# Idle transposes ahead of an attention kernel, replaced by full-float products in six tile forms

## The chip, the cores and the metric

The kernel runs on one core of one Trainium2 chip. The time is device microseconds of one execution. A core has TensorE (PE, the matrix array, with weight loads PEld), VectorE (DVE), ScalarE (ACT), GpSimd (POOL) and SyncE (SP, which issues DMAs here); each has its own queue of instructions.

## The reference

A pre-layernorm block on x of 2048 rows by 512: attention with 32 heads of 16, one key and one value head for all of them, and then a gated FFN of width 1792.

```
x  = A_x
q  = (LN(x) @ wq) in 32 heads of 16;  k = LN(x) @ wk;  v = LN(x) @ wv      # one k, one v
p  = softmax(q k^T / 4);  o = p v;   h  = x + concat(o) @ wo
h2 = h + (gelu(LN(h) @ w_gate) * (LN(h) @ w_up)) @ w_down
```

All inputs and the output are float32.

## The kernel before, in words

Rows are handled as 16 tiles of 128 (index t) and as 4 blocks of 512 (index b). The program has two parts.

The **prologue** (function `prologue`) makes keys, values and the first queries. For each tile t it goes round several engines:

- `stats(t)`: mean and variance on VectorE, the factor and shift from them by three small operations on GpSimd;
- `normalize(t)`: ScalarE writes xn, the normalised tile;
- `turn(t)`: TensorE transposes xn in four pieces of 128x128 into a PSUM tile `pt`; ScalarE copies it to `xT_hi` in a rounded float type (float32r), VectorE writes the rest of the rounding to `xT_lo`;
- `project_k` and `project_q` (through the generators `q_first` and `q_rest`): products of xT with the weights, in three terms (hi hi, lo hi, hi lo), into `pk` and `pq`.

`stats` runs three tiles ahead of `turn` and `normalize` two. Instructions of TensorE, GpSimd, ScalarE and, in the prologue, VectorE are queued in the order in which the code is written, so a place in the code is a place on the engine's queue. The list `IDLE` says how many *idle transposes* stand ahead of the turns of tiles 0 to 6: `turn(t)` first issues `IDLE[t]` transposes of the identity matrix into the same `pt`, whose result the real transposes then overwrite. After the sixteen turns come the last k projections, bounds for the softmax (`norm_k`, `max_k`), and the remaining q projections. Queries go through a DRAM array `q_d` to `qg_first`.

The **main part** scores 2048 keys against 512 queries of four heads at a time: `scores` makes s from kaug and qg (50 rows; the two matmuls of a step sit in rows 0 and 64 of the array), ScalarE takes the exponential p, and `weigh` adds p times v into `acc`, four heads on four column tiles of 32. p and v are plain float32 there; most other products have float32r operands. Later projections and the FFN are woven in between, as products on the two row halves of the array.

PSUM has eight banks of 512 floats; in the prologue `psum1` deals them out in turn (`width = 8`). `ident` is the 128x128 identity in float32, made on GpSimd; `v_sb` is a float32 array of 128x512 which VectorE fills with ones at the start and into which `leave_v` later writes v.

Of the kernel before, what the change touches and what calls it, by code (L numbers as in the profile page):

```python
# [19 lines left out]
P = 128  # L20
# [12 lines left out]
AHEAD_W = 2  # L33

LAST_Q = 258

LAG = 6

# [24 lines left out]
def kernel(  # L63
# [12 lines left out]
    nc = tc.nc  # L76
# [30 lines left out]
    ident = const.tile([P, P], F32, name="ident")  # L107
# [6 lines left out]
    v_sb = const.tile([P, KC, 2 * DH], F32, name="v_sb")  # L114
# [53 lines left out]
    def run(outer, first):  # L168
# [226 lines left out]
        if first:  # L395
            set_banks("ps_pro")
            width = 8
            order = tc.manual_schedule(engines={mybir.EngineType.DVE})
            with order:
                qg_first = prologue(  # L400
                    psum1, xT, wq_hi, wq_lo, sel, k2m, q_first, q_rest, advance,
                    first_q, first_bound, fill_first, eb
                )
# [670 lines left out]
        with tc.manual_schedule(engines={mybir.EngineType.SP, mybir.EngineType.DVE}):  # L1074
# [6 lines left out]
            while n < lead:  # L1081
# [6 lines left out]
                elif r < 30:  # L1088
                    kinds, runs = MIXED[r % 10]
                    if kinds == "ss" and 10 * left > 13 * (LAST_Q - n):  # L1090
                        kinds = "sm"
                    elif kinds == "mm" and 10 * left < 11 * (LAST_Q - n):
                        kinds = "sm"
                else:
                    kinds, runs = ("mm" if 10 * left > 13 * (LAST_Q - n) else "sm"), 1
                rest, held = token == REST, False
# [151 lines left out]
    def prologue(psum1, xT, wq_hi, wq_lo, sel, k2m, q_first, q_rest, advance, first_q, first_bound, fill_first, eb):  # L1248
        with ExitStack() as pro:
# [61 lines left out]
            nc.vector.memset(zero.bitcast(F32), 0.0)  # L1311
            nc.sync.dma_start(q_d[:, 3 * DH + 1, :].bitcast(F32), zero.bitcast(F32))

            def stats(t):
                st = sb.tile([P, 6], F32, tag="st", bufs=4, name=f"st_1_{t}")
                mv = sb.tile([P, 2], F32, tag="mv", bufs=4, name=f"mv_1_{t}")
                nc.vector.bn_stats(st, xs[t])
                nc.vector.bn_aggr(mv, st)
                rstd = sb.tile([P, 1], F32, tag="rstd", bufs=4, name=f"rstd_1_{t}")
                nc.gpsimd.tensor_scalar(rstd, mv[:, 1:2], EPS, None, op0=ALU.add)  # L1320
                nc.gpsimd.tensor_tensor(rstd, rstd, power[:, 0:1], op=ALU.pow)
                sh = sb.tile([P, 1], F32, tag="shift", bufs=4, name=f"shift_1_{t}")
                nc.gpsimd.tensor_scalar(
                    sh, mv[:, 0:1], rstd, -1.0, op0=ALU.mult, op1=ALU.mult
                )
                return sh, rstd
# [6 lines left out]
            def turn(t, xn):  # L1333
                pt = psum1(f"pt_{t}").rearrange("p (c q) -> p c q", c=DC)

                for k in range(IDLE[t] if t < len(IDLE) else 0):
                    nc.tensor.transpose(pt[:, k % DC, :], ident, ident)
# [59 lines left out]


            AHEAD, FIRST_FROM = 2, 6
            IDLE = (28, 3, 8, 9, 8, 12, 14)  # L1400
            sums, xns, pks, kss, vTs, pns, pvs = {}, {}, {}, {}, {}, {}, {}
            for t in range(AHEAD + 1):
                sums[t] = stats(t)
            for t in range(AHEAD):
                xns[t] = normalize(t, *sums.pop(t))
            for t in range(NT):
                if t + AHEAD + 1 < NT:
                    sums[t + AHEAD + 1] = stats(t + AHEAD + 1)
# [158 lines left out]
```

## Time and profile before

| | |
|---|---|
| timed runs | 1410.52 and 1411.73 us, median 1411.12 |
| profiled execution: span from first to last instruction | 1408.1 us (the page gives no time of its own around it) |
| mean granted TensorE clock | 0.996 |
| instructions | 25648 |
| TensorE busy | 1391.7 us, 99% |
| ScalarE busy | 1041.2 us, 74% |
| VectorE busy | 552.7 us, 39% |
| GpSimd busy | 189.4 us, 13% |

How the views read: a timeline row gives start, length, engine, line, operation, what it writes and from what, its shape and how many are merged (x28), and in brackets the engine's idle time just before it and what ended that. A chain row gives start, length and what the chain went through. A row of groups ends in busy time and mean nanoseconds of one. A row of windows gives a stretch, its length, and busy time of each engine with a count, then the granted clock (1.00 is full), the DMA engines' share and GB/s. A matmul on part of the array reads "50*128" for rows by columns.

### The profile page before, as it was taken

What the parts mean: (1) busy time and instruction counts of PE and PEld (TensorE: products, weight loads), DVE (VectorE), ACT (ScalarE), POOL (GpSimd) and SP (SyncE); (2) the same over time, 40 slices, a digit from 0 to 9 for tenths busy, and PEclk for the clock granted to TensorE, in tenths of its full rate; (3) what the DMA queues carried; (4) which work ended last, traced back from release to release, by engine and by line L of the source; (5) the groups of instructions that cost most, each with busy time, mean ns of one, the idle gap of its engine ahead of it and who ended that gap; (6) DMA issues with size and microseconds to landing.
All of it is one profiled execution on the core that took longest, in us unless ns stands there. A gap on an engine that the chain in (4) does not pass through costs nothing.

```text
span 1408.1 us, 25648 instructions
## 1 busy us (share of the span) xinstructions
PE 1391.7 (99%) x10646; PEld 782.7 (56%) x10646; DVE 552.7 (39%) x982; ACT 1041.2 (74%) x1149; POOL 189.4 (13%) x288
## 2 busy tenths in 40 slices
PE   8999999999999999999999999999999999999998
PEld 7433333335555555555555655555555555557886
DVE  7322323333342434333252433424352342427665
ACT  7699999996777787777787777777787777772000
POOL 6655565501000000000000000001000000002000
PEclk9999999999999999999999999999999999999999
DMA  4578777842341322233252332223242241335551
GB/s 160 162 238 273 236 243 243 298 134 91 126 150 53 124 106 102 73 112 122 84 169 72 117 118 87 87 100 111 99 151 97 88 147 56 134 124 198 181 199 59
DMA packets 85041, 194.52 MB, mean 138 GB/s; under 512 B 9904, under 2 KB 24240, under 8 KB 84884
## 3 DMA queue, kind: packets, MB, share of 16 engines
q1 hardware_dynamic: 77484, 167.39, 35.3%
q0 software_dynamic: 7264, 25.30, 5.0%
q8 instruction: 86, 1.41, 0.4%
q14 instruction: 39, 0.32, 0.1%
q10 hardware_dynamic: 168, 0.10, 0.0%
HBM read 142.93 MB, written 49.55 MB: 137 GB/s over the span
## 4 chain that ended last, share of the span: by engine, by line
PE 93%; ACT 3%; DMA 1%; issue 1%; DVE 1%; POOL 0%; SPq 0%; ACTq 0%; DVEq 0%; POOLq 0%
PE acc L439 33%; PE s L431 19%; PE pu L949 9%; PE pg L949 8%; PE pd L949 4%; PE pq L429 4%; PE pd L626 3%; ACT p L435 3%; PE pd L648 3%; PE pg L648 3%; PE pu L648 3%; PE pp L626 2%; PE pp L757 1%; DMA x<-in_A_x_dram 1%; PE pxt L693 1%
## 5 line engine op out<-in xcount | busy, mean ns | idle before, releaser
L435 ACT ACTIVATE p<-s 128x1024 f32<-128x1024 f32 x1024 | 969.7, 1030 | 224.6 <-PE s L431 220.1
L439 PE MATMUL acc<-p,v_sb 128*32 128x512 f32 x4096 | 496.4, 600 | 0.0
L431 PE MATMUL s<-qg,kaug 50*128 50x512 f32 x1984 | 416.3, 423 | 3.7 <-ACT p L435 3.6
L431 PEld LDWEIGHTS s<-qg,kaug 50*128 50x128 f32 x1984 | 194.6, 184 | 217.8 <-ACT p L435 120.6
L439 PEld LDWEIGHTS acc<-p,v_sb 128*32 128x32 f32 x4096 | 109.8, 109 | 229.2 <-issue 226.0
L949 PE MATMUL pu<-x2h,w 64*128 64x512 f32 x672 | 211.8, 391 | 0.0
L949 PE MATMUL pg<-x2h,w 64*128 64x512 f32 x672 | 211.5, 391 | 0.1
L949 PEld LDWEIGHTS pu<-x2h,w 64*128 64x128 f32 x672 | 115.8, 185 | 15.1
L949 PEld LDWEIGHTS pg<-x2h,w 64*128 64x128 f32 x672 | 116.2, 185 | 12.6 <-DVE g L823 0.5
L949 PE MATMUL pg<-x2l,w 64*128 64x512 f32 x336 | 122.2, 391 | 0.0
L949 PE MATMUL pu<-x2l,w 64*128 64x512 f32 x336 | 121.8, 390 | 0.0
L826 ACT ACTIVATE ga<-ga 128x512 f32<-128x512 f32 x56 | 35.3, 634 | 89.2 <-DVE ga L821 89.2
L139 POOL TENSOR_SCALAR rstd<-mv 128x1 f32<-128x1 f32 x16 | 3.5, 221 | 666.4 <-DVE mv L137 666.4
L949 PE MATMUL pd<-w,gh 64*128 64x512 f32 x384 | 81.3, 392 | 0.0
L891 DVE TENSOR_TENSOR h<-h,pd 128x512 f32<-128x512 f32 x48 | 31.9, 685 | 115.4 <-PE pd L949 66.4
L1192 DVE SCALAR_TENSOR_TENSOR ga<-ga,g 128x512 f32<-128x512 f32 x70 | 48.3, 691 | 52.3 <-ACT ga L826 51.2
L452 DVE COPY oT<-acc 128x512 f32<-128x512 f32 x32 | 22.1, 692 | 112.1 <-PE acc L439 111.9
L479 DVE RECIPROCAL oc<-oc 128x128 f32<-128x128 f32 x64 | 56.3, 921 | 24.3 <-DMA oc<-acc_d 19.5
L810 DVE COPY g<-pg 128x512 f32<-128x512 f32 x56 | 38.8, 692 | 62.8 <-PE pg L949 57.0
L949 PEld LDWEIGHTS pu<-x2l,w 64*128 64x128 f32 x336 | 57.9, 185 | 7.6
L949 PEld LDWEIGHTS pg<-x2l,w 64*128 64x128 f32 x336 | 58.1, 185 | 6.1
L823 DVE SCALAR_TENSOR_TENSOR g<-g,pu 128x512 f32<-128x512 f32 x56 | 38.2, 683 | 40.4 <-PE pu L949 30.4
(248 smaller groups left out, 1462.4 us busy)
## 6 DMA issues: line engine op xcount, KB each, us to landing
w<-w_d SPq DMA_DIRECT2D x112, 512.0 KB
w<-w_d SPq DMA_DIRECT2D x28, 1024.0 KB
qg<-q_d SPq DMA_DIRECT2D x46, 200.0 KB
q_d<-qh SPq DMA_DIRECT2D x32, 256.0 KB
wo<-wo_d SPq DMA_DIRECT2D x8, 1024.0 KB
acc_d<-oT SPq DMA_DIRECT2D x31, 256.0 KB
oc<-acc_d SPq DMA_DIRECT2D x124, 64.0 KB
w_d<-w_0b POOLq DMA_DIRECT2D x14, 512.0 KB, 7.6
```

The source lines that it names most:

```text
L429: step()
L431: nc.tensor.matmul(s[:, a, :], kaug[rows, kc * P : (kc + 1) * P], qg[rows, 2 * u + a, :], start=True, stop=True,)
L435: nc.scalar.activation(p[:, 2 * u : 2 * u + 2, :], s, AF.Exp, scale=SCALE)
L439: nc.tensor.matmul(acc[32 * j : 32 * j + 32, :], v_sb[:, kc, :], p[:, j, :], start=(kc == 0), stop=(kc == KC - 1), skip_group_check=True,)
L479: nc.vector.reciprocal(oc[:, 1, sl], oc[:, 1, sl])
L626: nc.tensor.matmul(banks[k], lhsT[rows], rhs[rows], start=(turn == 0 and i == 0), stop=(turn == 1 and i == n - 1), skip_group_check=True,)
L648: nc.tensor.matmul(bank, lhsT, rhs, start=(i == 0), stop=(i == len(ts) - 1))
L810: nc.vector.tensor_copy(g, pg)
L823: nc.vector.scalar_tensor_tensor(g, g, 0.5, pu, op0=ALU.mult, op1=ALU.mult)
L826: nc.scalar.activation(a, a, AF.Tanh, scale=GELU_A * GELU_C)
L949: nc.tensor.matmul(e["bank"], lhsT[rows], rhs[rows], start=i == 0 and not e["both"], stop=last and e["both"], skip_group_check=True,)
L1192: (soon or lazy).pop(0)()
```

## The change

`IDLE` becomes empty, so no `turn` issues idle transposes any more. In their place one block, `idle_products`, stands ahead of the loop over tiles. It takes eight PSUM banks and multiplies a piece of the identity (float32, stationary) with rows of `v_sb` (float32, 512 moving columns, all ones at that time). Nothing reads the results. A form (nr, ncol) cuts the array into nr row tiles and ncol column tiles; each row tile writes to a bank of its own, counted from `first`, each column tile to its own partitions of it.

```
+IDLE_FORMS = (
+    (1, 1, 4, 0), (2, 1, 4, 0), (1, 4, 3, 2), (4, 1, 3, 4), (4, 4, 3, 4), (1, 4, 2, 3),
+    (2, 4, 2, 0), (1, 1, 2, 3),
+)
...
+            def idle_products():
+                banks = [psum1(f"idle_{k}") for k in range(8)]
+                ones_f = v_sb.rearrange("p k d -> p (k d)")
+
+                def product(k, rows, cols):
+                    nc.tensor.matmul(
+                        banks[k][cols, :], ident[rows, cols], ones_f[rows, :],
+                        start=True, stop=True, skip_group_check=True,
+                    )
+
+                def tiles(nr, ncol, times, first):
+                    for _ in range(times):
+                        for r in range(nr):
+                            for j in range(ncol):
+                                h, w = P // nr, P // ncol
+                                product(
+                                    first + r, slice(r * h, (r + 1) * h),
+                                    slice(j * w, (j + 1) * w),
+                                )
+
+                for nr, ncol, times, first in IDLE_FORMS:
+                    tiles(nr, ncol, times, first)
...
             AHEAD, FIRST_FROM = 2, 6
-            IDLE = (28, 3, 8, 9, 8, 12, 14)
+            IDLE = ()
+            idle_products()
```

The eight entries give 4 + 8 + 12 + 12 + 48 + 8 + 16 + 2 = 110 products instead of 82 transposes. The line numbers below the block move by 5 to 29: 1337 (idle transposes) has no successor, 1339 (turn) becomes 1367, 431 (scores) 436 and 439 (weigh) 444; the products are on line 1324.

On TensorE, at the start of the program, before; pt_0 to pt_2 are the turned tiles 0 to 2, xn_0 to xn_2 their sources:

```order
L1337 MATMUL pt_0_213<-ident_60 128x128 [waits Pool_49]
L1337 MATMUL pt_0_213<-ident_60 128x128 x27
L1339 MATMUL pt_0_213<-ident_60,xn_0_200 128x128 [waits Activation_49]
L1339 MATMUL pt_0_213<-ident_60,xn_0_200 128x128 x3
L1337 MATMUL pt_1_259<-ident_60 128x128 x3
L1339 MATMUL pt_1_259<-ident_60,xn_1_202 128x128 [waits Activation_49]
L1339 MATMUL pt_1_259<-ident_60,xn_1_202 128x128 x3
L1337 MATMUL pt_2_280<-ident_60 128x128 x8
```

On TensorE at the same place after the change, from the end of the block on (the last 4x4 round's last row tile, 1x4, 2x4, 1x1), and then the first turns:

```order
L1324 MATMUL idle_7_180<-v_sb_69,ident_60 32x512 x4
L1324 MATMUL idle_3_176<-v_sb_69,ident_60 32x512 x8
L1324 MATMUL idle_0_173<-v_sb_69,ident_60 32x512 x4
L1324 MATMUL idle_1_174<-v_sb_69,ident_60 32x512 x4
L1324 MATMUL idle_0_173<-v_sb_69,ident_60 32x512 x4
L1324 MATMUL idle_1_174<-v_sb_69,ident_60 32x512 x4
L1324 MATMUL idle_3_176<-v_sb_69,ident_60 128x512 x2
L1367 MATMUL pt_0_331<-ident_60,xn_0_318 128x128 [waits PE_49,Activation_49]
L1367 MATMUL pt_0_331<-ident_60,xn_0_318 128x128 x3
L1367 MATMUL pt_1_349<-ident_60,xn_1_320 128x128 [waits PE_49,Activation_49]
```

The whole block stands ahead of the first turn, and nothing idle stands between the turns. The first product of the block waits for VectorE (the fill of v_sb) beside GpSimd (ident).

On TensorE where the seventh tile is turned and the first k projection begins, after the change; before, 14 idle transposes stood between the third and the fourth of these rows:

```order
L1377 MATMUL pk_0_446<-xT_hi_0_106,wk_hi_153 128x512 [waits PE_49,Activation_49]
L1377 MATMUL pk_0_446<-xT_lo_0_107,wk_hi_153 128x512 [waits DVE_49]
L1377 MATMUL pk_0_446<-xT_hi_0_106,wk_lo_154 128x512 [waits DVE_49]
L1367 MATMUL pt_6_459<-ident_60,xn_6_422 128x128 [waits PE_49,Activation_49]
L1367 MATMUL pt_6_459<-ident_60,xn_6_422 128x128 x3
```

Here only the idle ones are gone; the order of the real instructions is the same, and so it is on VectorE, ScalarE, GpSimd and SP.

## The prediction

> **What bounds the kernel now.** I read the page's head first, then the chain that ended last around the seam between the prologue and the attention, then the first 15 us in order of time.
>
> ```profile
> span 1408.1 us, 25648 instructions
> PE 1391.7 (99%) x10646; PEld 782.7 (56%) x10646; DVE 552.7 (39%) x982; ACT 1041.2 (74%) x1149; POOL 189.4 (13%) x288
> ...
> PE 93%; ACT 3%; DMA 1%; issue 1%; DVE 1%; POOL 0%; SPq 0%; ACTq 0%; DVEq 0%; POOLq 0%
> ```
>
> TensorE is busy for 99% of the span and carries 93% of the chain. Behind the prologue no slack is left that could swallow a late start: what the first score matmul loses, the end loses.
>
> ```profile
> 33.43 0.71 ACT xn L1330
> 34.13 0.04 issue
> 34.18 0.66 PE pt L1339 x4
> ...
> 46.83 3.51 PE pq L223 x15
> 50.35 0.02 issue
> ...
> 50.43 0.61 ACT pq_raw L242
> 51.03 0.04 issue
> 51.08 0.58 PE s L431 x2
> ```
>
> At 34.18 the sixteenth x tile is turned. From there to 50.35 the chain is TensorE back to back, and the first scores start at 51.08. So the question is when the sixteen turns are through, and that hangs on the first of them.
>
> ```profile
> 1.53 5.24 PE L1337 MATMUL pt<-ident 128*128 128x128 f32 x28 [1.53 <-POOL ident masks.py:199]
> ...
> 1.63 0.48 DVE L1308 MEMSET v_sb<- 128x512 f32 x1
> ...
> 7.25 0.66 PE L1339 MATMUL pt<-ident,xn 128*128 128x128 f32 x4 [0.49 <-ACT xn L1330]
> ...
> 7.71 0.81 ACT L1330 ACTIVATE xn<-x,shift,rstd 128x512 f32<-128x512 f32 x1 [0.51 <-DMA wq_raw<-in_A_wq_dram]
> ...
> 8.43 0.58 ACT L127 ACTIVATE xT_hi<-pt 128x512 fp32r<-128x512 f32 x1
> ...
> 13.42 1.47 PE L1337 MATMUL pt<-ident 128*128 128x128 f32 x12
> ...
> 14.73 0.60 PE L1339 MATMUL pt<-ident,xn 128*128 128x128 f32 x4
> ```
>
> Today the 28 idle transposes end at 6.77 and TensorE still waits 0.49 us for ScalarE: they cover a wait of 5.7 us (1.53 to 7.25) and delay nothing. They also show the clock. Twelve idle transposes at 13.42 take 1.31 us, 0.109 each. With that pitch 28 would take 3.2 us; they take 5.24. If the first n run at half rate, 27 pitches in 5.24 - 0.27 us (0.27 is the last one's own length, 1.47 - 11 x 0.109) give n = 18.6, which ends at 1.53 + 18.6 x 0.218 = **5.59 us**: until then the array is cold.
>
> **What the block of products costs.** All 110 products stand ahead of the first real turn on TensorE's queue, and the first waits for v_sb's fill (1.63 + 0.48 = 2.11) and so starts near 2.17. The nearest operation in the trace is line 439, the weighing: both operands full floats, 512 moving columns, four column tiles of 32.
>
> ```profile
> L439 PE MATMUL acc<-p,v_sb 128*32 128x512 f32 x4096 | 496.4, 600 | 0.0
> ...
> L949 PE MATMUL pu<-x2h,w 64*128 64x512 f32 x672 | 211.8, 391 | 0.0
> ```
>
> The code issues 4 x 8 x 16 x 4 = 2048 such matmuls, the trace has 4096: each full float product is two passes. One pass takes 600 ns against 391 for a rounded-float one with as many columns: 209 ns more. The length of such passes side by side follows from the chain:
>
> ```profile
> 84.83 1.85 PE acc L439 x16
> ...
> 323.98 2.71 PE acc L439 x24
> ```
>
> Eight passes more cost 0.86 us. So four products on four column tiles take 0.86 us, a **round**; one pass is 0.43, and a block has 0.13 us of its own (1.85 - 2 x 0.86) for getting in and out. A pass of 0.43 is twice the 0.215 that 512 columns need at the other rate; I take it that a lone 128x128 product also takes two passes of 0.43, for its tile is the same length in the moving direction.
>
> Rounds, if every tile of a form works beside the others: 4 (1x1) + 4 (2x1) + 3 (1x4) + 3 (4x1) + 3 (4x4) + 2 (1x4) + 2 (2x4) + 2 (1x1) = 23 rounds, 23 x 0.86 = 19.8 us. To it come:
>
> - the cold stretch, 2.17 to 5.59 at half rate. Line 439 shows the price of cold in the rows below: 8 passes take 1.86 us (58.38 to 60.24) at clock 0.50, 16 take 1.85 (61.61 to 63.46) at 1.00. So 3.42 us of cold do 1.71 us of work: +1.7.
> - 7 changes of form at 0.13: +0.9.
> - weights of 128 columns: the pq chain above has 15 passes in 3.51, 0.234 each against 0.215; 26 such pass slots (1x1, 2x1, 4x1) at 0.02: +0.5.
>
> ```profile
> 58.38 1.93 PE L439 MATMUL acc<-p,v_sb 128*32 128x512 f32 x8
> 60.24 0.50 PE L429 MATMUL pq<-xT_hi,wq_hi 64*128 64x512 f32 x1
> 60.25 0.50 PE L431 MATMUL s<-qg_first,kaug 50*128 50x512 f32 x1
> 60.58 0.39 PE L429 MATMUL pq<-xT_lo,wq_hi 64*128 64x512 f32 x1
> 60.59 0.40 PE L431 MATMUL s<-qg_first,kaug 50*128 50x512 f32 x1
> ...
> 61.61 1.92 PE L439 MATMUL acc<-p,v_sb 128*32 128x512 f32 x16
> 63.46 0.50 PE L431 MATMUL s<-qg_first,kaug 50*128 50x512 f32 x2
> ```
> ```profile
> 57.00:59.00 2.00, 2.00 (x12) 0.50 0.52 190
> 61.00:63.00 2.00, 2.00 (x22) 1.00 0.78 300
> ```
>
> The block ends at 2.17 + 19.8 + 1.7 + 0.9 + 0.5 = **25.1 us**, and the first real turn starts there instead of at 7.25: 17.8 us later.
>
> The Trainium skill ("TensorE: Matmul & The Clock Gate", Part 1) says that the gate opens after one busy window of about 3.4 us and that these windows run free of the kernel; by that the cold stretch could last up to 6.8 us and the term be 3.4 instead of 1.7. The profiled run opened 4.06 us after its first transpose (5.59 - 1.53), inside that span.
>
> **Do row tiles run side by side?** The trace has no product on four row tiles and none on 16. The two row halves do run together: pq on 64 rows and s on 50 start 0.01 us apart, and the next pair follows 0.34 us behind, not two passes behind. Bounds for a round on several row tiles: side by side as there (0.86), or one row tile after the other (0.86 for each). I take the first, since both the pair above and the four column tiles of line 439 go that way.
>
> **What is removed, and what comes back.** The 54 other idle transposes (3, 8, 9, 8, 12, 14) leave: 54 x 0.109 = 5.9 us of TensorE, all ahead of turns that wait for ScalarE's xn anyway. What paces the sixteen turns is the loop through the other engines:
>
> ```profile
> 7.25:34.18 26.93, 25.16 (x163) 20.51 (x163) 21.90 (x51) 22.77 (x38) 19.65 (x47) 1.00 0.43 152
> ```
> ```profile
> DVE st L1317 <- DMA x<-in_A_x_dram: 0.6, 1, 0.6
> ```
>
> Busy here are TensorE, weight loads, VectorE, ScalarE and GpSimd in this order. ScalarE works 22.77 of 26.93 us, so at most 4.2 us can be caught up. Loads are no cause: VectorE waits for x only 0.6 us once. The rest of ScalarE's waits are for GpSimd and VectorE, which do the same work in the same order as before. While the products run these three can only do what needs no turn: xn 0 and 1, statistics 0 to 3; then VectorE stands at xT_lo 0, ScalarE at xT_hi 0, and SP's x loads behind the tenth come as their buffers go free. The one sure gain: today xT_hi of tile 0 starts at 8.43, behind the second xn, though its turn ended at 7.91; now xn 1 is long done. **0.5 us** come back, at most 4.2; I take 0.5.
>
> **Sum.** 17.8 - 0.5 = **+17.3 us**. On the span that is 1408.1 + 17.3 = 1425.4; the page gives no time around the span, and the median of the timed runs, 1411.1, lies 3.0 above it. On the median: **1428**, 1.2% slower. A measurement of this kernel tells no difference under 2%, 28 us, so this counts as the same.
>
> **Rivals.**
>
> 1. *Row tiles one after the other* (the slow side). Extra rounds: 2x1 four, 4x1 nine, 4x4 nine, 2x4 two = 24, x 0.86 = +20.6: **1449**, 2.7% slower. It decides from about 13 extra rounds on. For it: no full-float product on row tiles is in the trace. Against: the pq and s pair. Chance 0.09.
> 2. *Row tiles half beside each other.* If TensorE starts passes only in program order and the two passes of a product follow each other, the second holds up the next row tile's first, and each step over rows costs 0.43: 2x1 8 steps, 4x1 12, 4x4 12, 2x4 4, each form 0.43 more at its end. That is 3.87 + 5.59 + 5.59 + 2.15 = 17.2 instead of 10.3 us: +6.9, **1435**. A like price comes if the dense forms can't be issued fast enough. The fastest stream seen is 16 passes with 16 loads in 1.85 us, 0.058 an instruction; 4x4's 192 instructions would then take 11.1 instead of 2.6 us, +8.5: 1437. Chance of either 0.12. The Trainium skill (same page, Part 3, The mechanism) states such an order: matmuls are "strict FIFO, no reordering". Line 439's rows speak against a blocking second pass on column tiles: four products would take 2.15 us, and take 0.86. For row tiles no run here shows it.
> 3. *More is caught up, or the pause at the seam stays warm.* The whole 4.2 us of ScalarE's waits in the loop instead of 0.5 gives 1424.7. The clock of 0.50 at 57 to 59 comes behind the thin start of the scores; were the array warm there, the eight cold passes from 58.38 (1.86, warm 0.93) and as many ahead of them save at most 1.9: together down to **1422**. Chance 0.08.
> 4. *The change does nothing*, the products fitting into the 5.7 us of waiting. 110 products from 2.17 to 7.25 would be 0.046 each; the fastest row has 0.215 (0.86 for four). TensorE's order still lists all of them. Chance 0.02, 1411.
>
> **How the numbers follow.** The forecast, 1425 to 1431 (0.5 to 3 us caught up, a cold stretch of 3.4 to 6.8 us), has 0.69. With rivals 2 and 3 that is 0.89; the range 1422 to 1440 leaves out rivals 1 and 4. Slower by over 2% (over 1439.3): rival 1 and the upper rim of 2, 0.11. Faster by over 2% (under 1382.9): no case reaches it, since nothing behind the seam gets shorter; 0.02. Same: 0.87.
>
> **What would show it.** In the changed profile line 1324 should have 220 passes, in a block from about 2.2 to 25; four products of the 1x4 form per 0.86 us; the 4x4 form through in 2.6 us (5.6 for rival 2, 10.3 for rival 1); the first turn on line 1367 at 25; the first scores on line 436 near 68.4 instead of 51.08; and from there to the end the same 1357 us as today (1408.1 - 51.08). Clock below 1.00 only at the start and for some 7 us at the seam. I am wrong if the scores start before 62 or behind 80, or if what follows them changes length by more than 3 us.

## The result, and the profile after

The changed kernel takes **1430.49 us** (1430.32 to 1430.66, 2 runs) beside 1411.12 us (1410.52 to 1411.73, 2 runs): a ratio of 1.0142, 95% interval 1.0112 to 1.0171, 1.4% slower. That is inside the range, 2.5 us above the forecast of 1428, and under the 2% that count as a difference. The page's head:

```profile
span 1428.6 us, 25932 instructions
PE 1407.7 (99%) x10784; PEld 779.1 (55%) x10784; DVE 547.3 (38%) x982; ACT 1041.3 (73%) x1149; POOL 189.2 (13%) x288
```

TensorE has 138 matmuls more (220 passes in, 82 transposes out) and is busy 16.0 us longer in a span 20.5 us longer. Where the 20.5 us enter is seen in the changed kernel's chain of work from the start to the first scores:

```profile
2.26 24.78 PE idle L1324 x215
27.04 0.45 PE pt L1367 x4
...
27.51 0.61 ACT xT_hi L132
...
53.30 0.66 PE pt L1367 x4
...
65.95 3.51 PE pq L228 x15
...
69.55 0.61 ACT pq_raw L247
...
70.20 0.58 PE s L436 x2
```

The products are the chain for 24.78 us, and the turns follow them at once. The chain shows only the last of the turns that follow each other directly; in order of time TensorE shows the first of them at 26.88, merged with the second, which no longer has to wait:

```profile
26.88 1.04 PE L1367 MATMUL pt<-ident,xn 128*128 128x128 f32 x8
28.86 0.66 PE L1367 MATMUL pt<-ident,xn 128*128 128x128 f32 x4 [0.95 <-ACT xn L1358]
```

Set beside the rows of before: the first turn 7.25 to 26.88 (+19.6), the sixteenth 34.18 to 53.30 (+19.1), the first scores 51.08 to 70.20 (+19.1). From there to the end it is 1358.4 us (1428.6 - 70.20) instead of 1357.0 (+1.4).

What a form takes is read from stretches for line 1324 alone. The first cut, 8.28, is where the passes turn fast; the others are the first passes of 1x4, 4x1, 4x4, 1x4, 2x4 and 1x1. The columns are the stretch, its length, PE's busy time and passes (counting one that runs in from before), PEld's, the clock, the DMA share and GB/s:

```profile
2.26:8.28 6.02, 6.02 (x7) 2.50 (x8) 1.00 0.97 291
8.28:12.49 4.21, 4.21 (x19) 1.47 (x17) 1.00 0.97 328
12.49:15.20 2.71, 2.71 (x26) 0.67 (x24) 1.00 1.06 396
15.20:17.99 2.79, 2.79 (x29) 1.14 (x25) 1.00 0.21 84
17.99:21.32 3.33, 3.33 (x100) 1.41 (x96) 1.00 0.03 7
21.32:23.18 1.86, 1.86 (x22) 0.42 (x17) 1.00 0.00 0
23.18:25.06 1.88, 1.88 (x37) 0.49 (x33) 1.00 0.00 0
25.06:26.88 1.82, 1.82 (x12) 0.67 (x4) 1.00 0.04 9
```

First row: seven passes in 6.02 us, 0.86 each, twice the warm 0.43. The clock column shows 1.00 there all the same: the profile has no clock recorded ahead of the first change, so the cold start has to be read from the lengths, here as in the kernel before. Third, fourth and fifth row: three rounds each of 1x4, 4x1 and 4x4 take 2.71, 2.79 and 3.33 us. Row tiles run beside each other; only the form with the most instructions is slower than the others.

### The profile page after: what moved, and what is told of

Read it like the earlier page. It is cut to its first block, busy times and chain, and to the rows that moved or that the text cites. A ratio compares the mean times of both kernels' runs of the same rounds, so it can differ in the third digit from the quotient of the medians.

```text
span 1428.6 us, 25932 instructions
## 1 busy us (share of the span) xinstructions
PE 1407.7 (99%) x10784; PEld 779.1 (55%) x10784; DVE 547.3 (38%) x982; ACT 1041.3 (73%) x1149; POOL 189.2 (13%) x288
## 4 chain that ended last, share of the span: by engine, by line
PE 94%; ACT 3%; DVE 1%; issue 1%; POOL 0%; DMA 0%; SPq 0%; ACTq 0%; DVEq 0%; POOLq 0%
PE acc L444 33%; PE s L436 19%; PE pu L954 8%; PE pg L954 8%; PE pd L954 5%; PE pq L434 4%; PE pd L631 3%; ACT p L440 3%; PE pd L653 3%; PE pg L653 3%; PE pu L653 3%; PE idle L1324 2%; PE pp L631 2%; PE pp L762 1%; PE pxt L698 1%
```

## The experiments

All of them compute the reference in full. The kernel before, run beside them, had medians of 1410.5 to 1411.5 us.

**The number of products.** Every form half as often, and twice as often.

```
 IDLE_FORMS, half:   (1,1,2,0) (2,1,2,0) (1,4,2,2) (4,1,2,4) (4,4,1,4) (1,4,1,3) (2,4,1,0) (1,1,1,3)
 IDLE_FORMS, double: every third number of the changed kernel's list times two
```

> The block cut to 12 of 23 rounds (one 4x4 round instead of three). Theory A: the block ends at 15.5 to 17.1 us (2.26 + 12 x 0.86 + 0.9 for the forms + 0.3 + 1.7 to 3.3 for the cold stretch), so the time is 1419 to 1420.5. Theory B, or a fixed price of having the block at all: nearer to 1430 than to 1420.

> The block with every count doubled, 46 rounds. Theory A: it ends near 47.5 us, the first turn is 40.2 us late, 0.5 come back: 1451. Theory B: below 1445, since what was taken away between the turns is lost only once.

Measured: half 1423.70 us (1420.88 to 1424.62; ratio 1.0086, 1.0069 to 1.0103), double 1449.85 (1448.68 to 1451.50; 1.0282, 1.0265 to 1.0299). Their blocks on TensorE, half first:

```profile
2.26 14.12 PE L1324 MATMUL idle<-v_sb,ident 128*128 128x512 f32 x102 [2.26 <-POOL sel L1299]
16.21 1.04 PE L1367 MATMUL pt<-ident,xn 128*128 128x128 f32 x8
```
```profile
2.26 44.87 PE L1324 MATMUL idle<-v_sb,ident 128*128 128x512 f32 x440 [2.26 <-POOL sel L1299]
46.96 1.04 PE L1367 MATMUL pt<-ident,xn 128*128 128x128 f32 x8
```

From products to first turn 12 rounds take 13.95 us, 23 take 24.62, 46 take 44.70: 0.97 and 0.87 us for each further round. Part of the difference is the cold start, which lasted 4.74, 6.02 and 5.51 us at half rate; without half of each it is 0.91 and 0.88. So the block's length is the sum of its rounds and of the cold start, and a first turn that is later by d makes the scores later by d - 0.5: 51.08 to 59.55 with half, to 90.25 with double. The double's time is 1 us from what was expected. **The half missed**: its median is 3 to 5 us longer than expected, and all of that arises behind the first scores, which stood where they should. Not every execution pays it: the shortest of the four took 1420.88, the profiled one, the longest, 1424.62.

**Where half the products lost 4 us.** Behind the first scores the profiled execution loses 4.5 us between the 192nd and the 256th exponential and 1.9 us in all that follows. In the first of these stretches TensorE has a wait that neither the kernel before nor the changed one has, and the windows around it show a clock that falls:

```profile
276.47 0.60 PE L436 MATMUL s<-qg,kaug 50*128 50x512 f32 x1 [1.75 <-DMA qg<-q_d]
```
```profile
260.00:270.00 10.00, 10.00 (x82) 3.75 (x80) 0.61 (x2) 9.88 (x11) 7.88 (x11) 1.00 0.79 261
270.00:280.00 10.00, 8.26 (x54) 3.37 (x50) 2.71 (x4) 7.28 (x9) 4.22 (x6) 0.83 0.82 261
```

The q of the next head group comes late, TensorE stands 1.75 us, and a stretch of 3.4 us at half clock follows (276.66 to 280.07), whose lost work is another 1.7 us. SP had issued that load at 265.84, 11 us ahead; in the changed kernel the same load goes out at 267.00, but the scores that need it stand 11 us later there:

```profile
265.84 1.71 SPq L416 DMA_DIRECT2D qg<-q_d  x2
```
```profile
267.00 1.05 SPq L416 DMA_DIRECT2D qg<-q_d  x2
```

The exponentials' starts tell how far such a load runs ahead of its group. For the seventh and eighth head group it is 16 to 19 us in the kernel before, the changed one and the double, and 12 to 14 with the twelve rounds below, none of which waits; it is 9.5 to 11 for at least one of the two in the half, in the 16-bit version, in the version with block and idle transposes, and in the one with a warm seam, which all lose 2 to 5.4 us at this place. One counterexample: with three products in the block (below) the load of the eighth group went out 10.2 us ahead and came in time. So a lead of some 10 us is on the edge; what decides there whether the load comes in time is not shown.

**Other operands.** The same 110 products with 16-bit floats: a copy of the identity from GpSimd, of the ones from ScalarE (shortened).

```
-ones_f = v_sb.rearrange("p k d -> p (k d)")
+ident_r = sb.tile([P, P], BF16, name="ident_r")
+nc.gpsimd.tensor_copy(ident_r, ident)
+ones_r = sb.tile([P, T], BF16, name="ones_r")
+nc.scalar.activation(ones_r, v_sb.rearrange("p k d -> p (k d)"), AF.Copy)
...
-    banks[k][cols, :], ident[rows, cols], ones_f[rows, :],
+    banks[k][cols, :], ident_r[rows, cols], ones_r[rows, :],
```

> The same 110 products in the same six forms, with bfloat16 operands (copies of the identity and of the ones, made on GpSimd and ScalarE): one pass of 0.215 us each instead of two of 0.43. Theory A: the block ends at 11 to 12.3 us and the time is 1414 to 1416. If it is not the passes' length that costs but the number of products, the changes of form or the banks: near 1430.

```profile
4.10 7.60 PE L1327 MATMUL idle<-ones_r,ident_r 128*128 128x512 bf16 x108 [4.10 <-ACT ones_r L1324]
...
12.07 1.04 PE L1370 MATMUL pt<-ident,xn 128*128 128x128 f32 x8
```

1414.87 us (1414.32 to 1419.89; ratio 1.0032, 1.0017 to 1.0047), as expected. One pass in place of two, at double the rate: the block is 8.0 us instead of 24.6. So two thirds of the block's price are the full-float form; the number of products, the tiling, the changes of form and the banks are the same in both.

**No idle work, and little of it.** `IDLE = ()` in the kernel before without any block; and three full-float products (`IDLE_FORMS = ((1, 1, 3, 0),)`) in place of the first 28 transposes, with the later ones as before.

> The kernel before with no idle transposes and no products. Theory A (the block's length alone shifts the first turn, and with it the end): the first turn stays at 7.25 us, so the time is that of before, 1411 to 1414; the turns and the first k products run on a cold array, which the loop through ScalarE and VectorE hides nearly all of. Theory B (a good part of the 19 us comes from the idle work that was taken away between the turns, since the array goes cold there): 1416 or more.

> Three full-float products on the whole array (six passes) in place of the first 28 transposes, the later idle transposes as before. Theory A (the time follows from when the block lets the first turn go): six cold passes of 0.86 to 1.0 us end near 7.4 to 7.9, so the first turn moves by 0.1 to 0.7 us, of which 0.5 is caught up behind it: the scores start within 0.3 us of the kernel before, time 1410 to 1412. Theory B (full-float products cost the rest of the kernel something of their own, by power or by the clock): 3 us or more longer than the kernel before, 1414 or more.

Without idle work 1412.05 us (1410.04 to 1417.27; ratio 1.0012, 1.0000 to 1.0024): all 82 transposes together are worth 1.7 us, between nothing and 3.4. In the profiled execution the first scores start as early as before (51.11); the first 32 exponentials then fall 1.8 us behind those of before, at a seam that is at half clock for 10.2 us instead of 6.8. The first row is this kernel's seam, the second that of the kernel before:

```profile
53.86:64.10 10.24, 10.05 (x42) 3.18 (x46) 1.72 (x3) 8.01 (x9) 5.35 (x7) 0.50 0.63 205
```
```profile
53.37:60.20 6.83, 6.35 (x24) 1.47 (x24) 1.72 (x3) 5.91 (x7) 5.79 (x6) 0.50 0.53 181
```

The three products: 1411.31 us (1409.34 to 1414.20; ratio 1.0003, 0.9993 to 1.0013).

```profile
2.26 4.77 PE L1321 MATMUL idle<-v_sb,ident 128*128 128x512 f32 x6 [2.26 <-POOL sel L1296]
7.26 0.66 PE L1364 MATMUL pt<-ident,xn 128*128 128x128 f32 x4 [0.23 <-ACT xn L1355]
```

Six passes end 0.23 us before xn 0 is there, the turn starts at 7.26 and nothing is lost. What costs is only what sticks out of the wait.

**The dense form by itself.** Twelve rounds of 4x4 as the whole block.

```
+IDLE_FORMS = ((4, 4, 12, 4),)
```

> The block is twelve rounds of the 4x4 form alone (192 products of 32 rows and 32 columns, 384 passes), the later idle transposes stay away. Theory A (the sixteen tiles run beside each other, but PE starts only one instruction in 16.7 ns, so that a round of 32 weight loads and 32 passes takes 64 x 16.7 ns = 1.07 us): 2.26 + 12 x 1.07 + 1.7 to 3.0 of cold, first turn at 16.8 to 18.4, cold lost in part since the issue is the limit and not the array; time 1420 to 1424. Theory B (tiles beside each other and 0.86 a round, the slow 4x4 stretch of the changed kernel being a matter of the changes of form around it): first turn at 14.3 to 15.6, time 1418 to 1421. Theory C (row tiles one after the other): 12 x 3.44 us, first turn near 44, time near 1448.

```profile
2.26 14.45 PE L1321 MATMUL idle<-v_sb,ident 32*32 32x512 f32 x351 [2.26 <-POOL sel L1296]
17.04 1.47 PE L1321 MATMUL idle<-v_sb,ident 32*32 32x512 f32 x33 [0.33 <-issue]
18.44 1.09 PE L1364 MATMUL pt<-ident,xn 128*128 128x128 f32 x8
```

1420.59 us (1420.04 to 1423.67; ratio 1.0074, 1.0053 to 1.0094), first turn at 18.44: row tiles one after the other (first turn near 44) are out. The starts of the rounds, 32 passes each, are 1.68, 1.71 and 1.71 us apart while cold, and from the fifth on (8.73) 1.04, 1.04, 1.04, 1.04, 1.04, 1.06. Cold, the array is the limit: two passes of 0.85. Warm, it would need 0.86 a round, as four column tiles do; 64 instructions (32 weight loads, 32 passes) in 1.04 us are 16 ns each, close to theory A's 1.07 a round. That the supply of instructions is what limits there is argued, but the changed kernel's trace speaks for it: the first of its three 4x4 rounds starts its passes 6.6 ns apart and is through in 0.88 us (17.99 to 18.87), as though its instructions had been waiting; the second takes 1.07, with many of its passes 16.7 ns apart.

**The removed later transposes.** The changed kernel with `IDLE = (0, 3, 8, 9, 8, 12, 14)`.

> The block of the changed kernel, and the later idle transposes (3, 8, 9, 8, 12, 14) put back. Theory A (the removed later transposes lay beside ScalarE's work and cost and brought nothing; the cold window behind the block falls on waits): first turn at 26.9, scores at 70.2, no window below clock 1.00 between 28 and 70, time that of the changed kernel within 1 us, 1429.5 to 1431.5. Theory B (without them the array cools between the turns and that costs part of the 19 us): scores start 1 us or more earlier, time 1429 or less.

1430.53 us (1428.36 to 1433.13; ratio 1.0132, 1.0112 to 1.0151). That is theory A's time, but not by its way. The profiled execution, the longest of the four, has the scores 1.3 us earlier than the changed kernel, which was theory B's sign; yet the first turn, too, came 1.3 us earlier (25.57 and not 26.88), since the array was warm already at 5.67, ahead of any of the transposes put back. Four passes in 3.41 us, then twice as fast:

```profile
2.26:5.67 3.41, 3.41 (x4) 1.48 (x5) 1.00 1.00 260
5.67:7.38 1.71, 1.71 (x5) 0.57 (x3) 1.00 0.99 370
```

The changed kernel has a half-clock stretch behind the block, where the turns wait for ScalarE and TensorE has little to do; with the transposes back it is gone, and at the seam there was none either. Windows of the changed kernel, then the same stretches of this one:

```profile
32.00:34.00 2.00, 1.47 (x6) 1.07 (x7) 1.90 (x9) 1.78 (x4) 0.84 (x4) 0.54 0.51 184
...
76.00:78.00 2.00, 2.00 (x12) 0.70 (x12) 0.08 (x1) 1.27 (x2) 2.00 (x3) 0.50 0.51 190
```
```profile
32.00:34.00 2.00, 2.00 (x16) 1.59 (x15) 1.99 (x5) 1.72 (x4) 1.50 (x3) 1.00 0.64 198
...
76.00:78.00 2.00, 1.93 (x14) 0.85 (x14) 1.62 (x3) 2.00 (x4) 0.98 (x2) 1.00 0.57 201
```

From the first turn to the first scores it is 43.29 us (25.57 to 68.86) beside 43.32 in the changed kernel: the stretch at half clock between the turns cost nothing. The warm seam won 1.8 us over the first 32 exponentials; the late qg loads took 5.4 us back by the 256th.

**A warm seam on purpose.** The kernel before, with five idle transposes ahead of the first score and behind those of n = 2 to 5.

```
+seam = psum1("seam").rearrange("p (c q) -> p c q", c=TB) if first else None
+def fill_seam():
+    for k in range(5):
+        nc.tensor.transpose(seam[:, k % TB, :], ident, ident)
+if first:
+    fill_seam()
...
+                    if first and 2 <= n <= 5:
+                        fill_seam()
```

> The kernel before with 25 idle transposes more, five ahead of the first score and five behind the scores of n = 2 to 5, where the array stands idle most of the time today (the half clock from 53 to 60 us). Theory A (the pause stays warm): no window at half clock behind 50 us, and the sixteen passes that take 3.7 us there now take 1.9: 1409 to 1409.5, 1.5 to 2 us faster. Theory B (the scores there wait for DMA and ScalarE, the clock is no limit): 1411 within 0.5. Theory C (the transposes delay the scores): 1412 or more.

```profile
57.00:59.00 2.00, 2.00 (x16) 0.51 (x20) 0.69 (x2) 1.59 (x3) 2.00 (x3) 1.00 0.52 191
```

The window that ran at 0.50 before runs at 1.00 now. The first exponential is 0.6 us late (the five transposes stand in front of its scores), the 32nd 0.7 us early: 1.3 us won. Yet the median is 1412.34 us (1410.76 to 1421.54; ratio 1.0013, 1.0001 to 1.0025). Theory A's mechanism was seen, its time was not reached; in the profiled execution, the longest of the twelve, 5 us were lost at 237 us to a late qg and 4.6 more at 710 us. What the median executions lost is not on record in a trace.

**Can the late loads be mended?** Two attempts, each on the half and on the warm seam: all loads of qg on ScalarE's queue, behind the sixth key tile; or only those of the seventh and eighth group, behind the eighth.

```
-nc.sync.dma_start(qg[64 * a : 64 * a + KR, hs, :], ...)
+nc.scalar.dma_start(qg[64 * a : 64 * a + KR, hs, :], ...)       # or only: b == 0 and g >= 6
-if kc == 2 and b * NG + g + 1 < NB * NG:
+if kc == 6 and b * NG + g + 1 < NB * NG:                        # or 8 for the two loads
```

> The kernel with half the products, with one thing changed in the main part: the loads of qg, the q of the next head group, are issued on ScalarE's queue behind the sixth of the group's sixteen key tiles, and not on SP's queue behind the second. With half the products SP issued two of them only 10 to 12 us ahead of the first score that needs them (17 to 18 us in the kernel before), since SP stands behind GpSimd's part of the weights; the scores then waited 2.5 us for qg and a window at half clock followed. Theory A (the 4 us by which half the products missed their forecast are these late loads): each load is issued 19 us ahead, TensorE waits nowhere for qg, the scores to the end take 1357 to 1360 us instead of 1363.4, time 1418.5 to 1420.5. Theory B (the loads are slow for want of DMA bandwidth, however early they are issued): the waits stay, time 1422.5 to 1424.5. Theory C (the issues hold up ScalarE's exponentials): no wait for qg, but waits for ScalarE, time 1422 or more.

> The kernel before with the 25 idle transposes at the seam and the loads of qg issued on ScalarE's queue behind the sixth key tile. The transposes alone kept the array warm at the seam (the scores ran 0.68 us ahead of the kernel before there), but lost 1.5 to 5 us around 237 us to a late qg. Theory A (the gain is real and only the late load took it back): 1408.5 to 1410, 0.5 to 2 us faster than the kernel before. Theory B (something else in the main part takes it back too): 1410.5 to 1413. Theory C (the issues hold up ScalarE): above 1413.

> Half the products, and only the two loads of qg that came late there (the head groups 6 and 7 of the first 512 queries) issued on ScalarE's queue, behind the eighth key tile of the group before, 15 us ahead of their first score; all others as in the kernel with half the products. With all loads on that queue the stretch in question (scores 192 to 256) had no wait for qg and lost 0.4 us instead of 4.5, but ScalarE stood up to 9 us at an earlier load. Theory A (these two late loads are what half the products lost): no wait of TensorE for qg, the first 256 steps keep the 8.4 us they start with within 0.6, time 1419 to 1421. Theory B (what is won there is lost again by a hold-up of ScalarE, or at a later load): 1422.5 or more.

> The kernel before with the 25 idle transposes at the seam and the loads of qg of groups 6 and 7 issued on ScalarE's queue behind the eighth key tile. Theory A (warm seam worth 0.7 us, taken back by the late loads alone): offsets to the kernel before of -0.7 us from score 32 to score 256 within 0.6; time 1409.5 to 1411. Theory B (a hold-up elsewhere in the main part takes it back): 1411.5 to 1414.

All four came out slower: 1438.92 (1436.30 to 1442.33) and 1435.75 us (1432.74 to 1444.07) for the half, 1431.29 (1428.69 to 1433.12) and 1427.56 (1426.36 to 1428.44) with the warm seam; ratios 1.0197, 1.0170, 1.0144, 1.0117, each within 0.0021. ScalarE's queue in the half with two moved loads:

```profile
233.16 6.61 ACTq L416 DMA_DIRECT2D qg<-q_d  x2
239.87 3.77 ACT L440 ACTIVATE p<-s 128x1024 f32<-128x1024 f32 x4 [10.97 <-DMA w_1r<-in_B_w_up_dram]
```

ScalarE stands 11 us, 6.6 of them over the load's issue, and the exponentials behind it wait along (3.6 us more at the second moved load); the row puts the end of the wait down to a transfer of weights, w_1r. No TensorE wait for qg is left in any of the four, and with all loads moved the half lost only 0.4 us between the 192nd and the 256th exponential instead of 4.5. So the late load is what cost the half its 4 us, as far as that stretch shows. It is not a clean test: the hold-ups on ScalarE had put these exponentials 13 us later already, which gave every other load more time as well. ScalarE's queue is no place to mend it. Why SP's stream of loads is 8 us later against the scores in some kernels than in others, behind GpSimd's part of the weights, stays open.

## Why the prediction was right, point by point

- **What bounds.** Right: the start of the chain is lost in full at the end, by +19.1 us at the first scores and +20.5 at the end.
- **Rounds, 23 x 0.86.** Right for five forms: 2.71 us for three rounds of 1x4 (2.58 and a change), 2.79 for 4x1, 1.88 for two of 2x4. In 4x4 a round needs 1.04 to 1.07 us, and three of them cost 0.6 us more than 1x4's. This looks like rival 2's second form, limited by issue, at under a tenth of its 8.5 us: I priced it from a stream that was itself waiting for the array (0.058 us an instruction), and TensorE took one in 0.016 on average.
- **The cold term, 1.7.** This is the term that was mis-sized. 6.02 us at half rate cost 3.0 instead of 1.7. I carried over from the kernel before the *moment* of warming (5.59), as though it belonged to the kernel. It doesn't: four kernels whose TensorE starts with the same products at 2.26 were cold for 3.41 (block and idle), 4.74 (half), 5.51 (double) and 6.02 us (changed), and the half's block with moved loads for 5.4. The Trainium skill ("TensorE: Matmul & The Clock Gate", Part 1) has a window of 3413 ns that runs free of the kernel. My estimate from it, 3.4 to 6.8 us, agrees with all of these, and its upper end of +3.4 was nearer than my 1.7.
- **Row tiles.** Right: side by side. Starts in strict order, with the two passes of a product one behind the other as rival 2 had them, would have made the 4x1 stretch 5.6 us; it is 2.79, and the first passes of its four row tiles start 6.6 ns apart. The Trainium skill ("TensorE: Matmul & The Clock Gate", Part 3, The mechanism) states a strict order for matmuls. If it is meant for the two passes of one product as well, this stretch does not bear it out; the trace does not name which pass belongs to which product.
- **What comes back, 0.5.** Right to 0.05: +19.62 at the first turn, +19.12 at the scores. ScalarE was free for xT_hi 0 at once (27.51, behind the turn). The other 3.7 us of ScalarE's waits were not caught up.
- **The same 1357 us behind it.** Not quite: 1358.4. 0.3 us go at the seam and 1.0 near 729 us, where one row half of the FFN products falls behind the other:

```profile
728.06 0.38 PE L954 MATMUL pg<-x2h,w 64*128 64x512 f32 x1
728.94 0.47 PE L954 MATMUL pu<-x2h,w 64*128 64x512 f32 x1 [0.50 <-DVE g L828]
```

  The experiments show that this part is no constant: 1356.7 us in the double, 1363.4 in the half. Executions of the kernel before differ by more than 1.4 us among themselves (1408.59 to 1415.40), so the 1.4 may be no effect of the change. That this part moved so little here is luck: no step of the prediction looked at how far ahead the loads run.
- **Clock.** The seam is cold as before; the half-clock stretch at 32 to 36 us I had not foreseen, though I had taken away the idle work that kept that place warm. Rival 3's price for a seam that stays warm, at most 1.9 us, was about right: block and idle gained 1.8 there.
- **The sum.** Start 0.1, cold 1.3, 4x4 0.6, the other terms -0.2: the first turn was 1.8 us later than the 25.1 forecast. The main part gave 1.4. Against that the execution is 1.7 us longer than its span (1430.32 beside 1428.6), not 3.0 longer as the median of before was against its trace. So the forecast is out by 2.5 us and not by more in part because these errors offset each other.

## What to carry to other kernels

Filler on an engine is free exactly as far as a wait ahead of it reaches: price it by passes times their length, and where it sticks out on a chain without slack it costs that in full, less what the next engine had queued. Don't carry a moment of warming from one trace to another kernel; give the cold start a range (3.4 to 6.0 us with the same first products here). And a kernel that is shifted as a whole isn't a constant plus the shift: look at how far ahead the loads run, for some 7 us less lead cost 2 to 5.4 us here.

## What was not expected of the hardware

- Through a long 4x4 stretch TensorE took one instruction in 16 ns (64 in 1.04 us). On four column tiles it does a round in 0.86 us, and a first 4x4 round in 0.88; over many 4x4 rounds the instructions seem to come too slowly for that.
- Between two rounds of 4x4 TensorE once started nothing for 0.92 us (the row at 17.04 with "issue" ahead of it); the trace names no cause.
- Cold starts with the same first products were 3.41 to 6.02 us long. The half-clock stretch at the seam, whose code is the same in all but the warm-seam kernels, was absent with block and idle, 3.4 us long with the twelve 4x4 rounds and with 16-bit floats, 6.8 before and in the changed kernel, the half, the double and the one with three products, and 10.2 without idle work. The 32nd exponential, measured from the first and set beside before, came 1.8 us earlier, 1.0 earlier, within 0.3, and 1.8 later: some 0.9 us for each 3.4. What decides the length is not shown.
- A wait of 1.75 us at full load was followed by 3.4 us at half clock (the half, 276.66 to 280.07); the 1.6 us wait in the warm-seam kernel (237.62) came with 6.8 us of it.
